# A ninth half tile of transposed keys in the room of the sixth ring slot, and a new pace for the MLP's steps

## The chip, the cores and the metric

One core of one Trainium2 chip. The metric is the device time in microseconds (us). The kernel before takes 1196.23 us (two runs, 1195.41 to 1197.05). Every experiment ran four times beside seven runs of the kernel before on the same chip, whose median was 1195.5 to 1197.2 us in each of the sets. A ratio is the mean time of a kernel's fast runs over that of the kernel before's fast runs of the same rounds, so it is not quite the ratio of the medians that stand beside it; brackets give its 95% interval.

## The reference, cut to what matters

Two layers, and both use the same key and value caches. That is why keys kept on chip from layer 0 save a read in layer 1.

```python
B, Sq, D = 8, 1, 448
Hq, Hkv, Sk, Dh = 16, 8, 4096, 256          # k_cache, v_cache: (8, 8, 4096, 256) bf16
x = A_x
for _ in range(2):
    x = x + attention(layernorm(x), k_cache, v_cache, wq, wo)   # two query heads share a key head
    x = x + block(layernorm(x), w3, w4)   # its input, plus: layernorm, w3, gelu, w4 of it
```

With one position per sequence the shifted mixing in the block contributes nothing, so the kernel needs only w3 and w4. One head's keys are 2 MiB, its values 2 MiB. All heads of both layers would be 512 MiB; this is a problem of reading.

## The kernel before

Keys and values of a (layer, batch, head) come in halves of 1 MiB through a ring of six slots, all issued in one order by SyncE. TensorE transposes keys (a "turn" is four transposes), VectorE and ScalarE copy the result out of PSUM (the memory that TensorE's results land in), TensorE makes the scores and, one head later, the product with the values. A slot is free, and the next read is issued, when TensorE has read the slot.

Eight half tiles of transposed keys (heads 0 to 3) stay on chip from layer 0 to layer 1. Each of the eight periods has a *stretch* of heads with nothing kept, then a *shared group*, in which layer 1 of batch b and layer 0 of batch b+1 alternate over the kept heads:

```python
full = N_KEEP // 2
part = N_KEEP % 2
kept_heads = full + part
A  = lambda b: [(0, b, h) for h in range(kept_heads, HKV)]
Bk = lambda b: [(0, b, h) for h in range(kept_heads)]
C  = lambda b: [(1, b, h) for h in range(kept_heads)]
Dn = lambda b: [(1, b, h) for h in range(kept_heads, HKV)]
first  = [p_ for b in range(1, B) for p_ in A(b)]
second = [p_ for b in range(B - 1) for p_ in Dn(b)]
per = (len(first) + len(second)) / B
# ... each period: per heads of first and second, then C(b)[i], Bk(b + 1)[i] in turn
```

Layer 1 of batch b can't begin before the batch's MLP and its new queries are done (`drain()` finishes them where they are not). That chain, `mix` and then `queries`, is a generator. A `pump()` stands after each turn, each two scores and each product with values, 14 points in a head, and advances it:

```python
def step():
    if jobs:
        n = len(S.ops["pe"])
        # ... next(jobs[0]), or drop the finished job
        return 1.0 if len(S.ops["pe"]) > n else 0.4     # a step with matmuls, or without
    return 1.0

def pump():
    credit["n"] = min(1.0, credit["n"] + credit["rate"]) if jobs else 0.0
    if credit["n"] > 0.0:
        credit["n"] -= step()
# when a batch has finished layer 0:
credit["rate"] = 0.80
jobs.append(mix(b, 1, True))
```

The layernorm is some 26 small VectorE operations in a row, cut by bare `yield`s into steps without matmuls. Each such step before the projection that needs its result lets one pump point of attention pass:

```python
def layernorm(lo, n, twice):
    # ... square, reduce; GpSimd: partition_all_reduce
    yield
    yield
    # ... mean, variance (5 operations)
    yield
    # ... centre; rsqrt: 3 operations, yield, then three Newton steps of 3 operations, each with a yield
# in mix():
    yield from layernorm(lo, n, True)
    scaled(lnT, r_ln, 1, n)
    # ...
    yield
    yield
    for ts in (range(0, 2), range(2, 4), range(4, 7), range(7, 9), range(9, 11), range(11, 14)):
        project(w3_cols, w3_r, C_H, ts, ts[0] >= NF // 2, n)     # TensorE waits for lnT
        # ...
        yield
```

Key copies out of PSUM: turns 1, 3, 5, 7 of a head on ScalarE (`ON_ACT`), the others on VectorE, in the same queue as the layernorm.

Of the kernel before, what the change touches and what calls it, by code (L numbers as in the profile page):

```python
# [18 lines left out]
GELU_K = 0.7978845608028654  # L19
RSQRT_MAGIC = 0x5F3759DF  # L20

N_RING = 6
N_KTR = 4
N_TK = 4
N_KEEP = 8
N_REP = 24
N_MLP = 24
N_PS = 2


# [19 lines left out]
class Sched:  # L50
# [8 lines left out]
    def op(self, eng, fn, reads=(), writes=(), dma=None):  # L59
        o = Op()  # L60
        o.eng, o.fn, o.inc, o.sem, o.amount = eng, fn, False, None, 1
        deps = []
        for r in reads:
            if r.w is not None:
                deps.append((r.w, "raw"))
        for r in writes:
            if r.w is not None:
                deps.append((r.w, "waw"))
            deps += [(t, "war") for t in r.r]
        known = self.known[eng]  # L70
        o.waits = []
        need = {}
        for t, kind in deps:
            if t.key == eng and (eng == "pe" or kind == "war"):
                continue
            if known.get(t.key, -1) >= t.idx:
                continue
            if t.key not in need or need[t.key].idx < t.idx:
                need[t.key] = t
        for t in sorted(need.values(), key=lambda t: -len(t.clock)):  # L80
            if known.get(t.key, -1) >= t.idx:
                continue
            o.waits.append(t)
            t.op.inc = True
            for k, v in t.clock.items():
                if known.get(k, -1) < v:
                    known[k] = v
            known[t.key] = max(known.get(t.key, -1), t.idx)
        if dma is None:
            key, idx = eng, len(self.ops[eng])  # L90
        else:
            key = ("dma", dma)
            idx = self.dsem.setdefault(dma, 0)
            self.dsem[dma] += 1
            o.sem, o.amount, o.inc = dma, 16, True
        o.tok = Tok(key, idx, dict(known), o)
        self.ops[eng].append(o)
        for r in writes:
            r.w, r.r = o.tok, []
        for r in reads:  # L100
            r.r.append(o.tok)
        return o.tok
# [25 lines left out]
def decode_two_layers(nc, A_x, A_k_cache, A_v_cache, A_wq, A_wo, B_w3, B_w4, out):  # L128
# [10 lines left out]
    def sb(name, shape, dt):  # L139
        return nc.alloc_sbuf_tensor(name, shape, dt), Res()  # L140
# [8 lines left out]
    w4, r_w4 = sb("w4_sb", [P, NF, D], bf)  # L149
    ring = [sb(f"ring{i}", [P, HALF, DH], bf) for i in range(N_RING)]  # L150
    ktr = [sb(f"ktr{i}", [P, 4, P], f32) for i in range(N_KTR)]
    keep = [nc.alloc_sbuf_tensor(f"keep{i}", [P, HALF, P], f32) for i in range(N_KEEP)]
    r_keep = [[Res() for _ in range(4)] for _ in range(N_KEEP)]

# [21 lines left out]
    r_o = [Res() for _ in range(B)]  # L176
    pT = [sb(f"pT{i}", [P, NI, 2], bf) for i in range(N_PS)]
    pm = [sb(f"pm{i}", [P, 2], f32) for i in range(N_PS)]
    gm = [sb(f"gm{i}", [P, 2], f32) for i in range(N_PS)]
    nb_ = [sb(f"nb{i}", [P, 2], f32) for i in range(N_PS)]  # L180
    rs = [sb(f"rs{i}", [P, 2], f32) for i in range(N_PS)]
    dn = [sb(f"dn{i}", [P, 2], f32) for i in range(N_PS)]
    rc = [sb(f"rc{i}", [P, 2], f32) for i in range(N_PS)]
# [27 lines left out]
# [5 lines that stand above are left out]
    def kept(h, a):  # L216
        k = 2 * h + a
        return k if k < N_KEEP else None

# [6 lines left out]
    per = (len(first) + len(second)) / B  # L226
# [34 lines left out]
    def load_next():  # L261
        n = state["loaded"]
        if n >= len(chunks):
            return
        state["loaded"] = n + 1
        src, b, h, a = chunks[n]
        t, r = ring[n % N_RING]
        op("sp", lambda e: e.dma_start(
            t[:, :, :], src[b, h].rearrange("(m s) d -> m s d", m=P)[:, a * HALF:(a + 1) * HALF, :]),
           writes=[r], dma=f"ring{n % N_RING}")  # L270

# [3 lines left out]
    def load_rows(t, tf, src, name):  # L275
        parts = []
        w = src.shape[1] // 2
        for kc in range(1, KC):
            parts.append((t[:, kc - 1, :], src[row0(kc):row0(kc + 1), :]))
        for half in range(2):  # L280
            parts.append((tf[64 * half:64 * half + 64, :], src[0:64, w * half:w * half + w]))
        return [op("sp", lambda e, o=o, i=i: e.dma_start(o, i), writes=[Res()], dma=f"{name}{k}")
                for k, (o, i) in enumerate(parts)]

    def reads_of(parts):
        out_ = []
        for t in parts:
            q = Res()
            q.w = t
            out_.append(q)  # L290
        return out_
# [4 lines left out]
    wq_r = reads_of(load_rows(wq, wqf, A_wq, "wq"))  # L296
    for _ in range(2, N_RING):
        load_next()
# [72 lines left out]
    def copies(cols, n):  # L371
        return cols.unsqueeze(1).to_broadcast([cols.shape[0], N_MLP // n, n])

    def room(w, at, n):

        r = N_MLP // n
        return mm[0:w, at:at + r * n].rearrange("p (r n) -> p r n", n=n)
# [49 lines left out]
    def outputs(lo, n, c, ts, first, alone):  # L427

        def f(e):
            w = kr(c)  # L430
            last = None
            for t in ts:
                at = C_Y + c * B + lo
                cols = oT[:, t // 2, t % 2, lo:lo + n]
                last = e.matmul(room(w, at, n) if alone else mm[0:w, at:at + n], wo[:, t, row0(c):row0(c) + w],  # L435
                                copies(cols, n) if alone else cols, start=first and t == ts[0],
                                stop=False, skip_group_check=True)
            return last
        op("pe", f, reads=[r_wo] + [r_o[b] for b in range(lo, lo + n)], writes=[r_mm])
# [58 lines left out]
    credit = {"n": 0.0, "rate": 1.0}  # L498
# [5 lines that stand above are left out]
            try:  # L504
                next(jobs[0])
            except StopIteration:
                jobs.pop(0)
            return 1.0 if len(S.ops["pe"]) > n else 0.4
        return 1.0

    def pump():
        credit["n"] = min(1.0, credit["n"] + credit["rate"]) if jobs else 0.0
        if credit["n"] > 0.0:
            credit["n"] -= step()

    def drain():
# [30 lines left out]
    def attend(g):  # L547
# [5 lines left out]
        def turn(f):  # L553

            a = f // 4
            n = index["k", g, a]
            src, r_src = ring[n % N_RING]
            bank, r_bank = tk[cnt["t"] % N_TK]
# [103 lines left out]
    def pv(g, a):  # L662

        q = g % N_PS
        n = index["v", g, a]
        v, r_v = ring[n % N_RING]

# [14 lines left out]
    def finish(g):  # L682

        layer, b, h = seq[g]
        q = g % N_PS

        def fn(e):
            last = None
            for c in range(2):
                last = e.transpose(pvb[:, DH + c * P:DH + (c + 1) * P], ob[:, c * P:(c + 1) * P], ident4[:, :])  # L690
            return last
        op("pe", fn, reads=[r_ob, r_ident4], writes=[r_pv])
        op("dve", lambda e: e.tensor_reduce(
            os_[:, :].rearrange("p (j c) -> p j c", c=2),
            pvb[:, DH:2 * DH].rearrange("p (c k w) -> p w c k", c=2, k=4)[:, 0:2, :, :],
            axis=AX.X, op=ALU.add), reads=[r_pv], writes=[r_os])
        op("dve", lambda e: e.tensor_tensor(  # L697
            oT[:, 2 * h:2 * h + 2, :, b], os_[:, :].rearrange("p (j c) -> p j c", c=2),
            rc[q][0][:, :].unsqueeze(2).to_broadcast([P, 2, 2]), ALU.mult),
           reads=[r_os, rc[q][1]], writes=[r_o[b]])  # L700
        after(g)
# [5 lines left out]
    def all_but(h):  # L707

        ts = [t for t in range(32) if t // 4 != h]
        for c in (1, 2, 3, 0):  # L710
            for n in range(0, 28, 14):
                outputs(B - 1, 1, c, ts[n:n + 14], c == 1 and n == 0, False)
                yield

    def after(g):

        layer, b, h = seq[g]
        if g == len(seq) - 2:
            jobs.append(all_but(seq[-1][2]))
        if last_of[layer, b] != g:  # L720
            return
        if layer == 0:
            credit["rate"] = 0.80
            jobs.append(mix(b, 1, True))
        elif b == B - 2:
            jobs.append(mix(0, B - 1, False))
        elif b == B - 1:
            for c in range(KC):
                outputs(B - 1, 1, c, range(4 * h, 4 * h + 4), False, False)
            jobs.append(mix(B - 1, 1, False, False))  # L730
# [89 lines left out]
```

## Time and profile before

| | before |
|---|---|
| time, median | 1196.23 us |
| TensorE / VectorE / ScalarE busy | 81% / 41% / 27% |
| ring transfers of 1 MiB | 256 of values, 192 of keys |
| DMA queue 1, share of 16 engines | 97.9% |
| mean granted TensorE clock | 0.925 |

Busy shares are averages over stretches and groups with different limits, so the prediction below reads them by window. Two views follow. The first is the page's row of TensorE's granted clock, in tenths, in 40 slices of 30 us:

```profile
PEclk8879989899999998999989899998999999899886
```

The second is who TensorE waits for inside a layernorm. The columns are microseconds in total, times, and the longest:

```profile
PE ps L598 <- DVE sm L324: 17.6, 20, 1.1
PE mm L405 <- DVE t L364: 13.1, 8, 5.0
...
PE mm L405 <- DVE lnT L364: 9.1, 1, 9.1
```

The reader is to see that each wait is short: 17.6 us over 20 waits, none above 1.1. (The 9.1, and the 5.0 in the row above it, belong to the start and the end of the kernel, where there is no attention to put in between.)

### The profile page before, as it was taken

How to read it: one execution, taken by the hardware profiler on the slowest of the kernel's cores; microseconds unless marked ns; L12 is line 12 of the kernel's file. 1: busy time of each engine (PE TensorE's matmuls, PEld its weight loads, DVE VectorE, ACT ScalarE, POOL GpSimd, SP SyncE). 2: the span in 40 equal slices, each digit the busy share in tenths (PEclk: the TensorE clock that was granted, in tenths of full speed). 3: DMA queues.
4: the chain of work that ended last, by engine and by line, in shares of the span. 5: the costliest groups of instructions: out<-in, count | busy, mean ns of one | idle time of the engine just before them, and what ended most of it. 6: DMA issues, size and time to landing. Idle time of an engine off the chain costs nothing.

```text
span 1196.6 us, 42443 instructions
## 1 busy us (share of the span) xinstructions
PE 963.4 (81%) x19195; PEld 842.2 (70%) x19195; DVE 485.2 (41%) x1707; ACT 320.9 (27%) x907; POOL 104.9 (9%) x281
## 2 busy tenths in 40 slices
PE   2767898788877888788977897788878897789895
PEld 2666787677766777677866886677767786678784
DVE  2323443335433443335433443335433443345253
ACT  1222322232222222232322322222322232223130
POOL 0000001101011001100110001000110011000100
PEclk8879989899999998999989899998999999899886
DMA  9999999999999999999999999999999999999992
GB/s 352 388 412 420 419 416 415 420 419 418 417 421 412 415 403 419 420 419 400 409 420 419 414 401 420 418 421 398 410 420 420 418 407 420 420 419 408 397 393 92
DMA packets 71828, 483.06 MB, mean 404 GB/s; under 512 B 7376, under 2 KB 13408, under 8 KB 13920
## 3 DMA queue, kind: packets, MB, share of 16 engines
q1 hardware_dynamic: 71648, 480.36, 97.9%
q8 instruction: 150, 2.46, 0.8%
q14 instruction: 30, 0.25, 0.0%
HBM read 480.32 MB, written 0.01 MB: 401 GB/s over the span
## 4 chain that ended last, share of the span: by engine, by line
DMA 44%; PE 39%; DVE 10%; issue 5%; POOL 1%; ACT 1%; SPq 0%; POOLq 0%; ACTq 0%
DMA ring<-in_A_k_cache_dram 44%; PE tk L574 21%; PE ps L598 6%; PE pvb L672 4%; PE mm L405 4%; DVE ktr L581 3%; PE mm L485 2%; PE mm L435 1%; PE pvb L690 1%; DVE sm L343 1%; ACT ktr L579 1%; DVE sm L325 1%; POOL gm L648 1%; DVE sm L326 1%; DVE ob L678 1%
## 5 line engine op out<-in xcount | busy, mean ns | idle before, releaser
L574 PE MATMUL tk<-ident,ring 128*128 128x128 f32 x3072 | 458.3, 298 | 121.9 <-DMA ring<-in_A_k_cache_dram 120.4
L574 PEld LDWEIGHTS tk<-ident,ring 128*128 128x128 f32 x3072 | 368.1, 152 | 160.4 <-DMA ring<-in_A_k_cache_dram 147.9
L581 DVE COPY ktr<-tk 128x512 f32<-128x512 f32 x256 | 176.7, 690 | 258.3 <-PE tk L574 257.6
L579 ACT COPY ktr<-tk 128x512 f32<-128x512 f32 x256 | 148.3, 586 | 358.3 <-PE tk L574 358.2
L672 PE MATMUL pvb<-ring,pT 128*2 128x256 bf16 x4096 | 161.7, 279 | 35.9 <-DMA ring<-in_A_v_cache_dram 28.5
L598 PE MATMUL ps<-qT,ktr 128*128 128x48 bf16 x4096 | 145.4, 184 | 22.6 <-DVE sm L324 17.6
L598 PEld LDWEIGHTS ps<-qT,ktr 128*128 128x128 bf16 x4096 | 130.5, 97 | 34.1 <-DVE ktr L581 26.0
L581 DVE COPY keep<-tk 128x512 f32<-128x512 f32 x128 | 88.5, 691 | 155.3 <-PE tk L574 154.7
L654 ACT ACTIVATE pT<-ps,nb 128x32 bf16<-128x32 f32 x256 | 76.4, 298 | 259.3 <-DVE nb L650 212.0
L598 PE MATMUL ps<-qT,keep 128*128 128x48 bf16 x4096 | 139.6, 186 | 5.1 <-issue 4.4
L598 PEld LDWEIGHTS ps<-qT,keep 128*128 128x128 bf16 x4096 | 130.4, 99 | 18.2 <-issue 10.3
L579 ACT COPY keep<-tk 128x512 f32<-128x512 f32 x128 | 75.0, 586 | 232.5 <-PE tk L574 232.5
L672 PEld LDWEIGHTS pvb<-ring,pT 128*2 128x2 bf16 x4096 | 76.0, 82 | 61.0 <-DMA ring<-in_A_v_cache_dram 35.2
L648 POOL PARTITION_ALL_REDUCE gm<-pm x128 | 45.4, 355 | 778.3 <-DVE pm L645 778.3
L678 DVE COPY ob<-pvb 128x256 f32<-128x256 f32 x128 | 53.7, 419 | 46.9 <-PE pvb L672 46.3
L659 POOL PARTITION_ALL_REDUCE dn<-rs x128 | 51.0, 399 | 150.9 <-ACT pT L654 150.9
L645 DVE TENSOR_REDUCE pm<-ps 128x2 f32<-128x64 f32 x128 | 28.6, 224 | 87.8 <-PE ps L598 87.8
L435 PE MATMUL mm<-oT,wo_sb 128*128 128x24 bf16 (+5 forms) x1280 | 60.6, 183 | 1.4 <-DVE oT L697 0.5
L435 PEld LDWEIGHTS mm<-oT,wo_sb 128*128 128x128 bf16 (+1 forms) x1280 | 51.3, 102 | 12.6 <-issue 9.1
L690 PE MATMUL pvb<-ident,ob 128*128 128x128 f32 x256 | 55.8, 302 | 2.8 <-DVE ob L678 1.6
L405 PE MATMUL mm<-lnT,wq_sb 128*128 128x24 bf16 x864 | 48.6, 184 | 10.5 <-DVE lnT L364 9.1
L405 PEld LDWEIGHTS mm<-lnT,wq_sb 128*128 128x128 bf16 x864 | 42.0, 99 | 19.2 <-DVE lnT L364 10.5
(65 smaller groups left out, 474.7 us busy)
## 6 DMA issues: line engine op xcount, KB each, us to landing
ring<-in_A_v_cache_dram SPq DMA_DIRECT2D x256, 1024.0 KB, 12.7
ring<-in_A_k_cache_dram SPq DMA_DIRECT2D x192, 1024.0 KB, 12.4
wo_sb<-in_A_wo_dram SPq DMA_DIRECT2D x1, 3584.0 KB, 26.8
wq_sb<-in_A_wq_dram SPq DMA_DIRECT2D x3, 1024.0 KB, 11.5
w_sb<-in_B_w_dram SPq DMA_DIRECT2D x1, 1568.0 KB, 22.8
w_sb<-in_B_w_dram SPq DMA_DIRECT2D x3, 448.0 KB, 14.3
wqf_sb<-in_A_wq_dram SPq DMA_DIRECT2D x2, 256.0 KB, 15.2
w3f_sb<-in_B_w_dram SPq DMA_DIRECT2D x2, 112.0 KB, 15.3
```

Source lines behind the costliest of these rows:

```text
L405: last = e.matmul(room(P, at + t * B, n), cols(kc, t), copies(rhs, n), start=(kc == 1), stop=(kc == 0), skip_group_check=True)
L435: last = e.matmul(room(w, at, n) if alone else mm[0:w, at:at + n], wo[:, t, row0(c):row0(c) + w], copies(cols, n) if alone else cols, star ...
L574: last = e.transpose(bank[:, j * P:(j + 1) * P], src[:, 4 * (f % 4) + j, :].bitcast(f32), ident4[:, :])
L579: op("act", lambda e: e.copy(flat, bank[:, :]), reads=[r_bank], writes=[r_kt])
L581: op("dve", lambda e: e.tensor_copy(flat, bank[:, :]), reads=[r_bank], writes=[r_kt])
L598: last = e.matmul(pst[:, at:at + 2 * N_REP].rearrange("p (r j) -> p r j", j=2), kt(i, c), repeated(qT[:, b, c, 2 * h:2 * h + 2]), start=(c ...
L648: op("pool", lambda e: e.partition_all_reduce(gm[q][0][:, :], pm[q][0][:, :], P, ReduceOp.max), reads=[pm[q][1]], writes=[gm[q][1]])
L654: return e.activation(pT[q][0][:, :, :].rearrange("p i j -> p j i")[:, j, :], pst[:, C_S:C_S + 2 * NI].rearrange("p (i j) -> p j i", j=2)[ ...
L659: op("pool", lambda e: e.partition_all_reduce(dn[q][0][:, :], rs[q][0][:, :], P, ReduceOp.add), reads=[rs[q][1]], writes=[dn[q][1]])
L672: last = e.matmul(pvb[at:at + 2, 0:DH], pT[q][0][:, a * HALF + i, :], v[:, i, :], start=(a == 0 and i < 4), stop=(a == 1 and i >= HALF - 4 ...
L678: op("dve", lambda e: e.tensor_copy(ob[:, :], pvb[:, 0:DH]), reads=[r_pv], writes=[r_ob])
L690: last = e.transpose(pvb[:, DH + c * P:DH + (c + 1) * P], ob[:, c * P:(c + 1) * P], ident4[:, :])
```

## The change

It gives the room of the sixth slot to a ninth kept half tile, so head 4's first half of keys is read once per batch and not twice. Five heads then take part in the shared groups, so the stretches have 5.25 heads on average in place of 7, and the MLP's steps are paced to fit. With `while`, one pump point runs steps as long as credit is left, so cheap steps (0.4 each) follow one another with no attention between them.

```diff
-N_RING = 6
+N_RING = 5
-N_KEEP = 8
+N_KEEP = 9
+CHAIN = 60
 def pump():
     credit["n"] = min(1.0, credit["n"] + credit["rate"]) if jobs else 0.0
-    if credit["n"] > 0.0:
+    while credit["n"] > 0.0:
         credit["n"] -= step()
-            credit["rate"] = 0.80
+            credit["rate"] = CHAIN / (14 * (per - 1))
```

## The prediction

> **What bounds the kernel now.** I read the page's slices and queues first. One core reads 480 MB; if the DMA engines never rest, nothing else can set the time.
>
> ```profile
> PE   2767898788877888788977897788878897789895
> ...
> DMA  9999999999999999999999999999999999999992
> GB/s 352 388 412 420 419 416 415 420 419 418 417 421 412 415 403 419 420 419 400 409 420 419 414 401 420 418 421 398 410 420 420 418 407 420 420 419 408 397 393 92
> ...
> q1 hardware_dynamic: 71648, 480.36, 97.9%
> ...
> ring<-in_A_v_cache_dram SPq DMA_DIRECT2D x256, 1024.0 KB, 12.7
> ring<-in_A_k_cache_dram SPq DMA_DIRECT2D x192, 1024.0 KB, 12.4
> ```
>
> The reader should see a DMA row of nines and a rate of 415 to 421 GB/s in most slices. 448 transfers of 1 MiB go through the ring. A transfer at 420 GB/s takes 1.0486 MB / 420 = 2.50 us; the landing records in the trace are 2.48 us apart, with a pause of about 1.5 us every 60 us. So 448 x 2.48 = 1111 us, plus 16 to 18 pauses (25), plus 10.4 MB of weights (25), plus start and tail (35 together), is the 1196 us. The landing takes 12.4 us, five transfers' worth: with six slots, a request finds about five ahead of it.
>
> Next, the waits and groups: who waits for whom.
>
> ```profile
> L574 PE MATMUL tk<-ident,ring 128*128 128x128 f32 x3072 | 458.3, 298 | 121.9 <-DMA ring<-in_A_k_cache_dram 120.4
> ...
> L672 PE MATMUL pvb<-ring,pT 128*2 128x256 bf16 x4096 | 161.7, 279 | 35.9 <-DMA ring<-in_A_v_cache_dram 28.5
> ```
>
> TensorE waits 149 us in all for data. But not everywhere. The busy times of windows show two regimes: 12 us of pure attention, 58 us in which a batch's MLP and next queries are mixed in, and the following 70 us, mostly with kept keys.
>
> ```profile
> 378.00:390.00 12.00, 9.18 (x162) 8.31 (x161) 5.40 (x13) 4.08 (x10) 0.88 (x3) 1.00 1.01 423
> 390.00:448.00 58.00, 51.69 (x1068) 44.99 (x1065) 27.12 (x108) 15.97 (x43) 4.56 (x12) 0.97 1.00 408
> 450.00:520.00 70.00, 52.88 (x1061) 45.77 (x1050) 25.04 (x78) 19.27 (x60) 7.53 (x20) 0.93 1.01 419
> ```
>
> The columns are the window, its length, busy us of PE, weight load, VectorE, ScalarE, GpSimd, then clock, DMA share and GB/s. PE is busy 77% of the first, 89% of the second (and stalled on VectorE in part of the rest), 76% of the third. In the middle one PE is slightly slower than the DMA. The DMA rides over it only because five transfers are queued.
>
> The timeline of one layernorm inside that window shows where PE loses time:
>
> ```profile
> 405.16 0.15 DVE L450 TENSOR_TENSOR xx<-mm,xx 128x4 f32<-128x4 f32 x1
> ...
> 405.81 0.40 POOL L339 PARTITION_ALL_REDUCE sm<-sm  x1 [7.01 <-DVE sm L335]
> ...
> 409.64 0.68 DVE L581 COPY ktr<-tk 128x512 f32<-128x512 f32 x1
> ...
> 410.39 0.57 PE L598 MATMUL ps<-qT,ktr 128*128 128x48 bf16 x16 [0.68 <-DVE sm L324]
> ...
> 411.89 0.17 DVE L364 TENSOR_TENSOR lnT<-xc,sm 128x4 bf16<-128x4 f32 x1
> ...
> 412.11 0.25 PE L405 MATMUL mm<-lnT,w_sb 128*128 128x24 bf16 x3 [1.16 <-DVE t L364]
> ```
>
> From the sum into x at 405.16 to the first projection at 412.11 is 7 us. PE stalls only 0.68 + 1.16 = 1.84 us of it, because attention work was placed in between.
>
> **What the Trainium skill says.** "DMA: Bandwidth & Descriptors", section Bandwidth, puts the fabric ceiling at 435 GB/s; the trace's 420 is near it, so fewer bytes is the only way to be quicker. The same page, "Anatomy of one DMA", gives each transfer a fixed cost of about 2 us beside its bytes, mostly the receipt before the semaphore fires (for the GpSimd path). The trace agrees for SyncE's: the first ring transfer, on an empty queue, landed 5.1 us after its issue, 2.5 of it data, so 2.6 fixed. "Perfetto Trace Analysis", section Optimizing Scalar/DVE Operations, gives a VectorE instruction on SBUF about 60 ns fixed cost, and about twice that as profiled latency; here a four-element operation takes 150 to 170 ns and the next starts some 0.19 us after it. So a layernorm is priced by its count of operations.
>
> **The change part by part.**
>
> (1) Ninth kept half tile. The fifth head's first half of keys is read in layer 0 and not again in layer 1: eight transfers less, one per batch. 8 x 2.48 = 19.8 us, with its share of the pauses 20. PE also drops 8 x 16 transposes and VectorE and ScalarE 16 copies each; PE waits for DMA there, so that is worth nothing more. Alone: 1196 - 20 = 1176.
>
> (2) Five slots in place of six. The room is equal (8 KiB a partition each). The rate is not touched while PE waits for data. What shrinks is how far PE may fall behind before the DMA runs dry. In pure attention a key transfer lands 12.8 us after its issue; with five slots that becomes 12.8 - 2.5 = 10.3. The DMA is dry at 5.1 (empty queue); 6.4 us occurs near 1134 and 1155 us with little loss, so I put dry at 5.6. The slack falls from 7.2 to 4.7 us.
>
> (3) The sequence. With five shared heads, the stretch between two shared groups has 5.25 heads on average instead of 7 (counted from the lists: 5,5,6,5,5,6,5,5). The MLP starts after the second head's first turns, so a stretch of five offers 10 + 3 x 14 = 52 pump points, 3.7 heads, where the MLP now takes 172 transposes / 32 = 5.4 heads.
>
> (4) The pump. The rate becomes 60 / (14 x 4.25) = 1.008, capped at 1 credit, and `if` becomes `while`. A step with a matmul costs 1, one without 0.4. There are 46 with (16 + 6 + 8 + 16) and some 23 without. Before, each step without took a point of its own: 46 / 0.8 + 23 = 80 at most, 75 measured (5.4 x 14). Afterwards 46 + 23 x 0.4 = 55 points: it just fits. But the nine empty steps of a layernorm, which were there to put attention between VectorE's chain and the projection, now take about 3 points instead of 9. One point is 7.6 / 14 = 0.54 us of PE work. Some 2 us instead of 5 cover a chain of 7 us, so the stall grows by about 2.7 us, twice per batch, and by about 0.9 at the gelu (one point instead of three): 6.3 us.
>
> **Sum for one stretch.** PE per streamed head without MLP: 9.18 / 12 x 9.92 = 7.6 us (9.92 us is four transfers). Before: 58 us less 1.1 of waiting for DMA is 57, less 5.4 x 7.6 = 41, leaves 16 us for the MLP with its stalls. DMA needed 5.4 x 9.92 = 53.5 us, so PE fell 3.5 us behind, inside the slack of 7.2. After: 3.7 x 7.6 + 16 + 6.3 = 50.4 us against 3.7 x 9.92 = 36.7: 13.7 us behind, against a slack of 4.7. The DMA rests 9 us in each of eight stretches, 72 us. The following shared group can't return this: the DMA already runs at full rate there. If half of the added stall is hidden (work shifts into it, less is queued on VectorE), 6 us a stretch, 47 in all. I take 7 us, 56 in all, a little under the full sum: 1196 - 20 + 56 = 1232; I predict 1230.
>
> **The rivals.** A: bytes alone count, the lag stays under the slack: 1176. For it: DMA at 97.9%, and PE's average load of 81% leaves room over a whole period. Against it: the ring bridges 5 us, a stretch is 50 us long, and the MLP's work is now denser by a third. B: the shorter ring and stretch matter, but the layernorm stalls don't grow: lag 3.7 x 7.6 + 16 - 36.7 = 7.4, dry for 2.7 us a stretch, 22 in all: 1198, no change. For it: VectorE is busy only 47% of the window, so the chain may get through sooner. C: the full sum, 1249. For it: VectorE works in order and has copies between, and PE too is in order, so nothing passes a waiting projection. I believe something between B and C.
>
> **Range and chances.** Low 1192: B with slightly more slack. High 1254: C with a further stall. 2% is 1172 and 1220. Faster needs more than all the bytes saved: 0.03. Within 2% holds A, B and weak forms of C: 0.35. Slower: 0.62.
>
> **What would show it.** Key transfers 184 instead of 192, landing at about 10 us: step 1 and 2. Dips in GB/s once a stretch to 300 to 350, and no dips in the shared groups: the dry DMA. PE's waits for the layernorm (scores after VectorE's sm 17.6 us, projections after t 13.1 us, 31 together) risen to 60 or more: step 4. SyncE's waits for slots still on PE. If GB/s stays at 415 and more throughout and the waits on layernorm don't rise, A is right and I am wrong; if the waits rise and GB/s doesn't fall, I have mis-sized the slack.

## The result, and the profile after

1261.28 us (two runs, 1258.35 and 1264.2), ratio 1.0544 [1.0434, 1.0653]: slower, by 65 us, though it reads 8.4 MB less. From the page of the changed kernel:

```profile
PE   2777887787886887877887888787777887787885
...
PEclk7879888888989989898889888897988988998886
DMA  8999989998999989999999989998999989998982
GB/s 316 378 415 420 374 322 398 420 404 295 384 419 419 371 335 421 419 419 355 358 421 419 378 307 418 421 419 308 399 420 420 401 319 421 420 414 295 362 312 122
...
q1 hardware_dynamic: 70496, 471.97, 93.5%
...
ring<-in_A_v_cache_dram SPq DMA_DIRECT2D x256, 1024.0 KB, 10.1
ring<-in_A_k_cache_dram SPq DMA_DIRECT2D x184, 1024.0 KB, 10.3
```

The reader is to see the row of GB/s: where it had stayed at 397 or more between start and end, it now dips to 295 to 358 about once per period of 140 us, and again near the end (312). The queue's share falls from 97.9% to 93.5%. Key transfers are 184 and take 10.3 us from issue to landing, 2.1 less than before; the ring has one slot (2.48 us) less. The granted clock's row has more eights than before; its mean fell to 0.885.

TensorE's waits for the layernorm, same columns as above:

```profile
PE mm L406 <- DVE lnT L365: 42.9, 10, 11.6
...
PE mm L406 <- DVE t L365: 31.3, 9, 5.0
...
PE mm L486 <- DVE hT L477: 10.1, 10, 1.5
```

Taken away 11.6 us at the start, the first two rows are 62.6 us, twice the 30.7 of before, and single waits are now 3.5 us. One of them, in the timeline (start, length, what, and in brackets the idle time before it and what ended it):

```profile
424.95 0.17 DVE L451 TENSOR_TENSOR xx<-mm,xx 128x4 f32<-128x4 f32 x1 [0.83 <-PE mm L436]
...
426.90 0.68 DVE L582 COPY ktr<-tk 128x512 f32<-128x512 f32 x1
...
430.18 0.18 DVE L365 TENSOR_TENSOR lnT<-xc,sm 128x4 bf16<-128x4 f32 x1
...
430.42 0.25 PE L406 MATMUL mm<-lnT,w_sb 128*128 128x24 bf16 x3 [3.49 <-DVE t L365]
...
430.86 1.11 PE L575 MATMUL tk<-ident,ring 128*128 128x128 f32 x4
```

From the sum into x at 424.95 to the projection at 430.42 is 5.5 us. Some 2 us of attention lie in between, and then TensorE stands for 3.49 us. In the last row four transposes take 1.11 us; at 420.56, before the wait, they took 0.63. The windows around that wait say why (window, length, busy us of PE, weight load, VectorE, ScalarE, GpSimd, then granted clock, DMA share, GB/s):

```profile
413.00:424.00 11.00, 10.84 (x249) 9.71 (x246) 3.90 (x11) 3.20 (x9) 0.75 (x2) 1.00 1.02 412
...
427.00:430.00 3.00, 0.00 (x0) 0.00 (x0) 2.58 (x16) 0.12 (x1) 0.00 (x0) 1.00 1.00 407
430.00:434.50 4.50, 4.08 (x90) 3.70 (x91) 1.54 (x7) 0.58 (x1) 0.35 (x1) 0.62 0.69 246
434.50:438.00 3.50, 2.59 (x45) 2.30 (x42) 2.54 (x9) 1.47 (x6) 0.40 (x1) 1.00 1.01 407
```

TensorE is idle from 427 to 430 while VectorE works; then the granted clock is 0.62 for the next window, and in that same window the DMA falls to 69% and 246 GB/s: by now TensorE is so late in freeing slots that the queue has run empty.

**Where the time went.** I took the landing of each of the 440 ring transfers from the trace and called "lost" what an interval between two landings has above 2.48 us. Before, 63.7 us are lost in all: 32.9 at the start, 29.9 in recurring pauses, 0.9 elsewhere. After, 150.1: 35.4 at the start, 27.9 in pauses, 66.5 in the first seven stretches (with 15 us after each, since landings come after issues), and 20.3 in the last stretch and the end. So the balance is -8 x 2.48 = -19.8 for the bytes, and +86.4 for DMA rest: +66.6, against 65.8 in the two profiled spans (1262.4 and 1196.6). Nearly all of it is lost at transfers that found less than 3.7 us of queued work ahead of them when issued.

### The profile page after: what moved, and what is told of

The parts are those of the page before. It is cut to its first block, busy times and chain, and to the rows that moved or that the text cites. A ratio compares the mean times of both kernels' runs of the same rounds, so it can differ in the third digit from the quotient of the medians.

```text
span 1262.4 us, 42152 instructions
## 1 busy us (share of the span) xinstructions
PE 975.7 (77%) x19067; PEld 857.2 (68%) x19067; DVE 483.6 (38%) x1691; ACT 314.7 (25%) x891; POOL 104.9 (8%) x281
## 3 DMA queue, kind: packets, MB, share of 16 engines
q1 hardware_dynamic: 70496, 471.97, 93.5%
## 4 chain that ended last, share of the span: by engine, by line
PE 44%; DMA 41%; DVE 9%; issue 4%; POOL 1%; SPq 1%; ACT 0%; POOLq 0%; ACTq 0%
DMA ring<-in_A_k_cache_dram 39%; PE tk L575 20%; PE ps L599 9%; PE pvb L673 5%; PE mm L406 4%; PE mm L436 2%; DMA ring<-in_A_v_cache_dram 2%; PE pvb L691 2%; DVE ktr L582 2%; PE mm L486 1%; SPq L269 1%; DVE sm L326 1%; DVE sm L327 1%; DVE sm L344 1%; DVE sm L325 1%
## 5 line engine op out<-in xcount | busy, mean ns | idle before, releaser
L582 DVE COPY ktr<-tk 128x512 f32<-128x512 f32 x224 | 154.6, 690 | 244.8 <-PE tk L575 244.3
L580 ACT COPY ktr<-tk 128x512 f32<-128x512 f32 x224 | 131.2, 586 | 404.4 <-PE tk L575 404.4
L582 DVE COPY keep<-tk 128x512 f32<-128x512 f32 x144 | 99.5, 691 | 170.2 <-PE tk L575 169.6
L599 PE MATMUL ps<-qT,keep 128*128 128x48 bf16 x4608 | 157.0, 187 | 5.6 <-DVE qT L423 3.6
L599 PEld LDWEIGHTS ps<-qT,keep 128*128 128x128 bf16 x4608 | 148.3, 99 | 17.7 <-issue 7.7
L580 ACT COPY keep<-tk 128x512 f32<-128x512 f32 x144 | 84.3, 586 | 266.3 <-PE tk L575 266.3
L599 PE MATMUL ps<-qT,ktr 128*128 128x48 bf16 x3584 | 135.4, 188 | 0.6
L599 PEld LDWEIGHTS ps<-qT,ktr 128*128 128x128 bf16 x3584 | 122.5, 100 | 6.7 <-ACT ktr L580 1.5
L691 PE MATMUL pvb<-ident,ob 128*128 128x128 f32 x256 | 58.4, 314 | 6.1 <-DVE ob L679 6.1
L436 PEld LDWEIGHTS mm<-oT,wo_sb 128*128 128x128 bf16 (+1 forms) x1280 | 52.1, 104 | 13.9 <-issue 10.1
## 6 DMA issues: line engine op xcount, KB each, us to landing
ring<-in_A_v_cache_dram SPq DMA_DIRECT2D x256, 1024.0 KB, 10.1
ring<-in_A_k_cache_dram SPq DMA_DIRECT2D x184, 1024.0 KB, 10.3
```

Of the source, the lines that this page charges most:

```text
L436: last = e.matmul(room(w, at, n) if alone else mm[0:w, at:at + n], wo[:, t, row0(c):row0(c) + w], copies(cols, n) if alone else cols, star ...
L580: op("act", lambda e: e.copy(flat, bank[:, :]), reads=[r_bank], writes=[r_kt])
L582: op("dve", lambda e: e.tensor_copy(flat, bank[:, :]), reads=[r_bank], writes=[r_kt])
L599: last = e.matmul(pst[:, at:at + 2 * N_REP].rearrange("p (r j) -> p r j", j=2), kt(i, c), repeated(qT[:, b, c, 2 * h:2 * h + 2]), start=(c ...
L691: last = e.transpose(pvb[:, DH + c * P:DH + (c + 1) * P], ob[:, c * P:(c + 1) * P], ident4[:, :])
```

## The experiments

For all of them I use two numbers from the traces. The **lag** is the length of the MLP's part of a stretch, less what the DMA needs for the heads transposed in it (9.92 us a head), mean of the first seven stretches: how far TensorE falls behind. **Dry** is the time lost at transfers that found less than 3.7 us of queue ahead. Theory 1 says that dry time comes when the lag exceeds the ring's slack; theory 2, that five outstanding transfers alone slow the DMA; theory 3, that the layernorm waits of the new pump reach the end by themselves.

Lag and dry are of the one profiled execution of each kernel, the medians of all its executions. The pump's rate is 0.80 where the table says so; else it follows the changed kernel's formula, 1.008 with nine tiles and 60/84 = 0.71 with eight (while_r6, r5_while); k9_spread has 1.0.

| kernel | slots | kept | pump | other edit | median us | ratio [95%] | lag | dry |
|---|---|---|---|---|---|---|---|---|
| before | 6 | 8 | if, 0.80 | | 1196 | 1 | 4.5 | 1 |
| r5_only | 5 | 8 | if, 0.80 | | 1203.1 | 1.0055 [1.0029, 1.0080] | 3.9 | 4 |
| while_r6 | 6 | 8 | while | | 1203.8 | 1.0058 [1.0040, 1.0077] | 5.8 | 2 |
| r5_while | 5 | 8 | while | | 1225.3 | 1.0249 [1.0218, 1.0280] | 5.5 | 18 |
| k9_r6_if | 6 | 9* | if | | 1193.9 | 0.9970 [0.9953, 0.9988] | 8.6 | 9 |
| k9_if | 5 | 9 | if | | 1210.4 | 1.0111 [1.0075, 1.0147] | 8.9 | 30 |
| k9_r6 | 6 | 9* | while | | 1236.4 | 1.0354 [1.0311, 1.0397] | 13.9 | 61 |
| k9_r8 | 8 | 9* | while | | 1196.3 | 0.9998 [0.9980, 1.0016] | 13.6 | 15 |
| after | 5 | 9 | while | | 1261.3 | 1.0544 [1.0434, 1.0653] | 14.6 | 87 |
| k9_ln1 | 5 | 9 | while | one Newton step | 1232.3 | 1.0305 [1.0288, 1.0323] | 10.9 | 51 |
| k9_warm | 5 | 9 | while | idle matmuls | 1254.2 | 1.0482 [1.0462, 1.0501] | 13.4 | 69 |
| k9_spread | 5 | 9 | prices turned | | 1216.3 | 1.0169 [1.0142, 1.0195] | 10.1 | 33 |
| k9_nowait | 5 | 9 | while | constant input* | 1257.4 | 1.0518 [1.0493, 1.0544] | 13.6 | 79 |
| k9_nowait2 | 5 | 9 | while | and no lift* | 1224.1 | 1.0240 [1.0217, 1.0263] | 9.9 | 40 |
| k9_nowait3 | 5 | 9 | while | and copies on ScalarE* | 1187.0 | 0.9917 [0.9895, 0.9938] | 5.2 | 10 |
| k9_if_ln1 | 5 | 9 | if | one Newton step | 1188.9 | 0.9927 [0.9911, 0.9944] | 5.7 | 12 |
| k9_if_ln1_act | 5 | 9 | if | and 6 of 8 copies on ScalarE | 1185.3 | 0.9906 [0.9878, 0.9935] | 5.1 | 10 |
| k9_if_ln1_act8 | 5 | 9 | if | and 8 of 8 | 1181.5 | 0.9875 [0.9856, 0.9895] | 4.4 | 5 |
| before_ln1_act | 6 | 8 | if, 0.80 | one Newton step, 6 of 8 | 1194.4 | 0.9987 [0.9971, 1.0004] | 3.3 | 0 |

A star marks a kernel that is wrong on purpose. The comparison with the reference passed all of them, the wrong ones too, so "correct" says little here.

### The parts one by one: r5_only, k9_if, while_r6, k9_r6

**r5_only**, the kernel before with five slots:

```diff
-N_RING = 6
+N_RING = 5
```

> The kernel before with five slots and nothing else changed (eight kept tiles, old pump). Theory 1 (TensorE's lag against the ring's slack): the lag of a stretch stays 4 to 6 us, the slack with five slots is about 4 (10.3 us from issue to landing, dry at about 6.3), so the DMA is dry 0 to 2 us a stretch, some 10 us in all: 1200 to 1210. Theory 2 (five outstanding transfers alone slow the DMA everywhere): most of the 66 us is here, plus the 20 us of bytes not saved: 1260 to 1285. Theory 3 (the layernorm stalls of the while pump are the cause): 1196, nothing.

Measured 1203.1 us. Its row of GB/s, to be held against that of the changed kernel:

```profile
GB/s 356 390 415 420 419 400 419 420 419 396 403 420 420 410 399 391 420 419 406 406 419 420 416 413 420 417 416 397 418 419 420 398 403 420 420 419 394 394 405 104
```

There are shallow dips (391 to 406) and none at 300. Five slots alone cost 7 us, in the range of theory 1, where theory 2 asked for 64 or more. Theory 2 falls.

**k9_if**, the changed kernel with the old conditional:

```diff
-    while credit["n"] > 0.0:
+    if credit["n"] > 0.0:
```

> The changed kernel with if in place of while in the pump: one empty step per point again, what is left over is drained. Theory 1: the added stall of some 4 us a stretch goes, over eight stretches and the tail about 30 us: 1225 to 1240. Theory 2: no change, 1260. Theory 3: the whole loss goes and the bytes show: 1176 to 1190.

Measured 1210.4: 51 us of the 65 are gone, more than theory 1 had expected (the lag fell by 5.7 us, not by the 4 of the waits alone), but the bytes still don't show. Theory 3 in its pure form is wrong too. The trace also shows what `if` does to a chain that no longer fits its stretch: in five of the first seven stretches the last 120 matmuls of the queries (15 of 16 steps) run in one block of 3.4 to 3.9 us at the end, left over for `drain()`, where the changed kernel has 24 in such a block. So this kernel keeps the layernorms spread and not the matmuls.

**while_r6**, the new pump with six slots and eight tiles:

```diff
-N_RING = 5
-N_KEEP = 9
+N_RING = 6
+N_KEEP = 8
```

> Six slots, eight kept tiles, only the new pump (while, rate 60/84 = 0.71). Theory 1: the lag of a stretch grows from about 4 to about 8 us against a slack of 6.5: dry 1 to 2 us a stretch, 1200 to 1210. Theory 2: 1196. Theory 3: 4 us of stall in each of eight stretches reach the end: 1225 to 1235.

Measured 1203.8: the same `while` that costs 51 us above costs 7 here, where the stretch is longer, the ring has a slot more and the rate is 0.71 in place of 1.008; this pair doesn't separate the three.

**k9_r6**, a sixth slot for the changed kernel. It doesn't fit in SBUF, so the ninth tile uses the first one's room:

```diff
-N_RING = 5
+N_RING = 6
-keep = [... for i in range(N_KEEP)]
+keep = [... for i in range(N_KEEP - 1)]
+keep.append(keep[0])          # and the same for r_keep
```

> The changed kernel with a sixth slot, which fits only because the ninth kept tile shares the room of the first (the result is wrong on purpose; times, transfers and instructions are those of the change). Theory 1: 2.5 us more slack in each of eight stretches and the tail, 20 to 25 us back: 1235 to 1242. Theory 2: all comes back, 1176 to 1182. Theory 3: nothing comes back, 1261.

Measured 1236.4: 25 us back for 2.5 us of slack in eight stretches. Theory 1's number.

### Threshold and dose: k9_r8, r5_while, k9_ln1, k9_spread

**k9_r8** has eight slots, with three shared tiles:

```diff
-N_RING = 5
+N_RING = 8
+keep += keep[:3]              # of six tiles; r_keep likewise
```

> The changed kernel with eight slots (three of the nine kept tiles share room with the first three; wrong result on purpose). Theory 1, lag against slack: the slack rises from about 4 to 11.5 us against a lag of about 14, so 2 to 3 us a stretch stay dry: 20 to 25 us over the floor of 1176, so 1192 to 1205. If instead the stalls themselves lengthened the whole and not by way of the ring, it would stay near the 1236 of six slots.

Measured 1196.3. The lag is still 13.6 us and TensorE's waits for the layernorm still stand (the three rows of the result differ by 2 us at most), but the DMA hardly feels them until the last slices:

```profile
GB/s 348 406 395 420 419 396 412 419 419 416 385 420 420 419 402 421 419 419 419 378 419 419 419 377 409 420 419 407 408 419 420 419 398 416 420 419 412 353 334 75
```

So a wait of TensorE costs nothing by itself; only what exceeds the ring's slack costs.

**r5_while** asks whether costs add or a threshold lies between:

```diff
-N_KEEP = 9
+N_KEEP = 8
```

> Five slots and the new pump, but eight kept tiles (the long stretch). Five slots alone cost 7 us and the pump alone 7. If the costs only add: 1210. Theory 1 has a threshold in it: six slots had some slack left that each change used up, so together they cost more than the sum: lag 7 us against a slack of 4, 3 us in each of eight stretches: 1218 to 1228.

Measured 1225.3. Five slots (7 us) and the pump (7 us) together cost 29, twice their sum. The pump costs 7, 29 - 7 = 22, 42 (1236.4 - 1193.9) and 51 us as slack and stretch shrink: a threshold. (The first two are at the rate of 0.71, against 0.80 with `if`.)

**k9_ln1** shortens the chain on VectorE by six operations a layernorm and keeps the pump's steps:

```diff
 for i in range(3):
+    if i > 0:
+        yield
+        continue
```

> The changed kernel with one Newton step in place of three in each inverse square root (six VectorE operations of some 0.19 us fewer in each layernorm; the steps of the pump are the same, the result slightly less exact). If the chain on VectorE behind the first projection is what TensorE waits for, each of two layernorms a batch is 1.1 us shorter, and in eight dry stretches and the tail all of it reaches the end: 15 to 25 us less, 1237 to 1246. If the loss of the while pump is in the bunching of its matmuls and not in the chain, nothing: 1258 to 1264.

Measured 1232.3, 29 us less, beyond the expected 15 to 25. The summed waits for VectorE of a stretch fell from 7.8 to 5.4 us as reckoned (12 x 0.19), the lag by 3.7. The rest goes with the clock: integrating 1 minus the granted clock over a stretch gives 6.6 us in the changed kernel and 3.9 here, part of it lying in the waits themselves.

**k9_spread** turns the prices of steps round:

```diff
-    return 1.0 if len(S.ops["pe"]) > n else 0.4
+    return 0.5 if len(S.ops["pe"]) > n else 1.0
-credit["rate"] = CHAIN / (14 * (per - 1))
+credit["rate"] = 1.0
```

> The changed kernel with the pump's prices turned round: two steps with matmuls at one point (0.5 each), one step without at each point (1.0), 46 points in all, so that the chain fits in a stretch of 52 points with the layernorms still spread. Theory 1: the added stall goes and nothing is left to drain; the lag falls to about 7 to 8 us against a slack of 4: 1200 to 1212, near or below the if variant's 1210. If matmuls bunched in pairs hurt, above 1215.

Measured 1216.3, a miss: the waits for VectorE fell to 4.5 us a stretch, but the chain was through after 3.1 heads, not the 3.6 of the changed kernel. The same MLP beside less streaming is a larger lag, some 1.2 us by an estimate (half a head, 9.92 us of DMA less the prediction's 7.6 of TensorE, for each head), of a lag of 10.1. The other reading, that matmuls in pairs hurt, is not excluded by this run alone; k9_nowait3 below speaks against it.

### The clock, the last corner and two attempts at a better kernel

**k9_warm** puts 96 matmuls of 24 columns ahead of a projection that waits:

```diff
+def warm(k):
+    # k times: matmul(mm[:, 440:464], ident, ident[:, 0:24])
 # in mix, and in queries for one batch, ahead of the projections:
+    warm(96)
```

> The changed kernel with 96 idle matmuls (24 columns, into unused columns) put ahead of each batch's first projection after a layernorm, where TensorE only waits for VectorE. They take about 2.7 us of a wait of 3.5. If the lower granted clock after each long stall (0.55 to 0.62 for some 4.5 us in the trace) is a part of the cost of its own, it goes: about 2 us at each of 16 stalls, 25 to 35 us less, 1226 to 1237. If the stall itself is the whole cost, nothing changes: 1258 to 1266.

Measured 1254.2: 7 us, where 25 to 35 were expected if the clock mattered and none if not. The timeline shows two stalls of one stretch:

```profile
421.14 2.55 PE L405 MATMUL mm<-ident 128*128 128x24 bf16 x96
...
424.42 0.65 PE L589 MATMUL tk<-ident,ring 128*128 128x128 f32 x4
...
438.66 2.55 PE L405 MATMUL mm<-ident 128*128 128x24 bf16 x96
442.30 0.25 PE L417 MATMUL mm<-lnT,wq_sb 128*128 128x24 bf16 x3 [1.08 <-DVE lnT L365]
...
442.75 1.11 PE L589 MATMUL tk<-ident,ring 128*128 128x128 f32 x4
```

After the first filler the transposes run at 0.65 us a turn; after the second, with an idle 1.08 us behind it, they are slow again, 1.11. In all, transposes of more than 400 ns within the first seven stretches are 145 of 804 in the changed kernel, 85 of 804 here and 20 of 848 in k9_if (counted beside the MLP). So the filler mended about half of what the new pump added to the slow clock. Whether the slow clock has a cost of its own stays open: the ratio here, 1.0482, lies inside the interval of the changed kernel's two runs (1.0434 to 1.0653), so the 7 us are not clear of the noise. If they are real, 7 us for 60 of 145 would make some 17 us for all, an estimate.

**k9_r6_if**: k9_r6 with `if` in the pump.

> Nine kept tiles (the ninth sharing room with the first, wrong on purpose), six slots, if in the pump: the last corner of the three parts. Lag about 8 us against a slack of 6.5: 1 to 2 us a stretch dry, over the floor of 1176: 1185 to 1195. If the costs of the parts only added (while 51, the sixth slot 25 against the change's 1261), 1185; if the short stretch by itself costs what 1210 minus 1176 shows whatever the ring, 1210.

Measured 1193.9, in the range, and the first with nine tiles that is clearly below the kernel before. Its profiled span (1188.8 us) shows 76.2 us lost in all, 12.5 more than before, of which 9 are dry queue; so of the 20 us of bytes some 7 arrive there.

**k9_if_ln1**: two edits on the changed kernel.

```diff
-    while credit["n"] > 0.0:
+    if credit["n"] > 0.0:
-    for i in range(3):          # Newton steps of the inverse square root
+    for i in range(1):
```

> The changed kernel with if in the pump and one Newton step (with its empty pump steps gone too, so less is left to drain). Attempt at a kernel that beats both. The lag of the if variant (7 to 8 us) falls by about 2 to 3: 3 to 4 us, at the slack of 4; what remains is the start and the last stretch: 1188 to 1198.

Measured 1188.9. **k9_if_ln1_act** adds `ON_ACT = (1, 2, 3, 5, 6, 7)`:

> The same, with six of the eight key copies of a head on ScalarE in place of four, so that fewer copies queue on VectorE behind and between a layernorm's operations. If what is left of the stall comes from that queue: 1182 to 1192. If ScalarE's copies of 0.59 us, three in four turns, now make TensorE wait for a bank, 1195 or more.

Measured 1185.3. Both are below the kernel before, as expected.

### Is the wait all of the pump's cost? k9_nowait, k9_nowait2, k9_nowait3

**k9_nowait** lets the projections of a single batch, and the lift of 64 rows behind the first one, read a constant tile that nothing writes, in place of `lnT`:

```diff
-    rhs = lnT[:, ...]
+    rhs = (fix if n == 1 else lnT)[:, ...]      # the same in lift(); reads r_fix in place of r_ln
```

> The changed kernel whose projections of a single batch read a constant tile in place of the layernorm's result (wrong on purpose; all VectorE work and all matmuls stay), so TensorE no longer waits for the layernorms. If waits for the layernorm, with the slow clock after them, are what the while pump costs, the lag falls from 14.6 to 4 or 5 us, near the slack: 1183 to 1197. If the denser matmuls of the new pump cost by themselves, 1210 (the if variant) or more.

Measured 1257.4: nothing, and taken at its word that would have refuted the waits. But the waits had not gone:

```profile
PE mm L408 <- DVE lnT L398: 59.4, 17, 4.7
```

The second projection now waited 3.6 us for VectorE's copy of the lifted rows. That copy reads the same PSUM bank, and it stands in VectorE's queue behind the whole layernorm. An in-order queue carries a wait to everything behind it.

**k9_nowait2** drops the lift and its copy for a single batch (`if n == 1: return`).

> As k9_nowait, which did not take the wait away: TensorE then waited 3.6 us for VectorE's copy of the lifted rows, which reads the same PSUM bank and stands behind the whole layernorm in VectorE's order. Here the lift and its copy go too for a single batch (wrong on purpose). If waits for the layernorm, with the slow clock after them, are what the while pump costs: lag 14.6 to 5 or 6 us, 1183 to 1200. If the denser matmuls of the new pump cost by themselves: 1210 or more.

Measured 1224.1, in the range of the second cause (1210 or more): by its number the density would be guilty. But the projection's wait is gone and a third way opened: the attention's own scores wait for key copies that stand behind the layernorm,

```profile
PE ps L604 <- DVE ktr L587: 32.0, 16, 2.8
```

which is some 4 us a stretch. **k9_nowait3** puts all eight key copies on ScalarE:

> As k9_nowait2, with all eight key copies of a head on ScalarE. In k9_nowait2 TensorE no longer waited for the projection's data but 4.2 us a stretch for key copies that stand behind the layernorm on VectorE. With both ways closed: if those waits are the rest of the while pump's cost, the lag falls from 9.9 to 5 or 6 us, 1190 to 1202. If ScalarE, now with all copies, holds TensorE back (0.59 us a copy against 0.68 us a turn), or the matmuls' density costs by itself: 1210 or more.

Measured 1187.0, a little below the expected range, with the `while` pump untouched; the remaining wait for copies is

```profile
PE ps L604 <- ACT ktr L585: 2.7, 7, 0.4
```

So the density of the matmuls costs nothing that shows. What the new pump cost was TensorE standing behind bunched VectorE work, by three ways, with the slower clock after it. One thing is missing: the same edits with the `if` pump were not run. They took away 74 us, more than the pump's 51, so they also mended waits that k9_if has, and a few us of density could hide behind that.

### The best version and its control

**k9_if_ln1_act8** is k9_if_ln1 with `ON_ACT = (0, 1, 2, 3, 4, 5, 6, 7)`.

> The best variant so far (if, one Newton step, six of eight copies on ScalarE, 1185) with all eight copies on ScalarE. If what is left (lag 5.1 us) still comes from copies behind the layernorm: 1180 to 1185. If ScalarE becomes the engine that TensorE waits for: 1188 or more.

Measured 1181.5, 1.2% below the kernel before, which is clear of the noise, and some 5.5 us above the floor of 1176 that the prediction had for the bytes alone. Its page:

```profile
PEclk8879998899899998999899998999889999999896
DMA  9999999999999999999999999999999999999992
GB/s 357 385 414 420 419 389 420 419 420 418 379 419 420 419 419 408 419 420 410 378 419 419 412 393 422 419 420 417 416 411 419 414 404 417 419 420 417 367 398 106
```

The DMA row is nines again; single slices at 367 to 393 remain. TensorE's waits for the layernorm are down to one each:

```profile
PE mm L406 <- DVE lnT L365: 7.3, 1, 7.3
...
PE mm L406 <- DVE t L365: 3.9, 1, 3.9
```

**before_ln1_act** is the control: the two edits of k9_if_ln1_act (except the pump, which is the old one there anyway) on the kernel before.

> The kernel before (six slots, eight kept tiles, old pump) with one Newton step and six of eight copies on ScalarE: the control for the 1185 us of the nine-tile kernel with the same two edits. If the ninth tile earns the gain there, this stays at the DMA's bound, 1192 to 1197. If the shorter layernorm and the copies earn it, 1184 to 1189.

Measured 1194.4, against 1185.3 with nine tiles and the same edits. The gain is the ninth tile's; the edits only let it through. (No control was run for the copies 8 of 8.) The control is bound by the DMA already, so shorter waits have little to give. One Newton step is a loss of accuracy, from rounding level to about 0.2% in the inverse square root by the formula, which whoever takes this version must accept; no run here tried two steps.

## Why the prediction was right or wrong

The direction and the mechanism were right, the time was outside the range: 1261, predicted 1230, range 1192 to 1254. By its own steps:

1. **The bytes** (-20 us). Right: 184 key transfers, and the rest of the balance closes with -19.8.
2. **The slack** (7.2 us to 4.7). Nearly right. Landing took 10.3 us as stated. Dry began a little earlier than 5.6 us from issue to landing: transfers that found less than about 3.7 us ahead of them, so about 6.2, already came late (in the changed kernel those that found 3.0 to 3.5 landed 3.1 us after the one before in the median, in place of 2.48). That makes the slack 4.1.
3. **The shorter stretch.** Right: 3.6 heads measured beside the MLP, 3.7 predicted. (That the chain "just fits" was not: by the prediction's own count it needs 55 points, and a stretch of five heads has 52. In those stretches the last 24 query matmuls run in a row at the end, in 0.8 us.)
4. **The pump.** The size was right, its terms were not, and that is luck. Added wait predicted 6.3 us a stretch; measured 7.8 in place of 3.9, so 3.9. Against k9_if, which has the same stretch and ring, the lag rose by 5.7: the waits for VectorE by 2.9 (4.9 to 7.8), the clock lost over a stretch by 3.9 (2.6 to 6.6), partly within the same waits. The clock was left out of the sum; that it fills the gap is read from the traces, and k9_warm didn't settle it. The Trainium skill, "TensorE: Matmul & The Clock Gate", in Part 1 on the HAM clock gate, says that the clock halves after an idle window of about 3.4 us and that the same time of activity brings it back. The trace agrees at this stall: 3.49 us idle, then 0.62 granted, turns of 1.11 us in place of 0.63. It also shows slow turns after shorter waits (last section). I had read the clock's row and not priced it.
5. **The lag** (13.7 us). Measured 14.6.
6. **From the lag to the time.** Here the prediction failed. Its full sum, rival C, had 9 us a stretch; I took 7, "if half of the added stall is hidden (work shifts into it, less is queued on VectorE)", a discount that no view of the profile supported. The first seven stretches lost 66.5 / 7 = 9.5 us each, where the measured lag less the measured slack is 14.6 - 4.1 = 10.5: hardly anything was hidden. And I priced the last stretch as one of eight equal ones; it and the end, with the MLP of the last batch and then that of the other seven batches together, where the shared group has values only, lost 20.3 us. Seven stretches at 9.5 for 7 are 17.5 us more, 20.3 for 7 in the last is 13, the start 2.5: 33 us on the sum of 1232, less 3 in the pauses and elsewhere, where the profiled run took 1262.

Of the rivals, A (bytes alone) is what k9_if_ln1_act8 nearly reaches, and B (waits that don't grow, 1198) is nearest to k9_if, with waits of 4.9 us a stretch: 1210. (Two small slips in the sums change nothing: the full sum C is 1176 + 72 = 1248, not 1249, and the weights are 10.6 MB, not 10.4.)

## What to carry to other kernels

In a kernel that the DMA bounds, a buffer slot is worth nothing until the consumer's longest lag needs it, and then each microsecond of missing slack is paid in every period: compare the lag of the worst stretch with the slack before trading a slot for bytes, and treat the end of the program as a stretch of its own. Where an in-order engine waits behind a chain of small operations, spread other work between, shorten the chain, or take unrelated work out of the queue behind it; and when an experiment that removes a wait changes nothing, look whether the wait is still there by another way. Don't discount a sum without a view that shows where the discount comes from.

## What the Trainium skill lacked or had wrong

- "TensorE: Matmul & The Clock Gate", Part 1, tells what brings the clock back, and that frequent short idles can make it swing, but not how thin activity may be. In k9_warm, 96 matmuls of 24 columns over 2.55 us, then 1.08 us idle, were followed by slow turns (1.11 us) at one stall, while the same filler, with 0.30 us idle after it, was followed by fast ones (0.65 us) at the other. And the kernel before has 97 of 1217 slow transposes beside the MLP in its first seven stretches, with no wait for VectorE above 1.2 us there (for data up to 1.9). The page has no measure by which to foresee these; whether its remark in Part 4, that transposes don't count as busy in the same way, bears on them, no run here tests.
- "DMA: Bandwidth & Descriptors" gives the fixed cost of a transfer, but not how much must be queued to keep the engines from resting. Here, on SyncE's queue with 1 MiB transfers, it was about 3.7 us of queued work (some one and a half transfers of 2.48 us); a transfer issued on an empty queue landed 5.0 us later.
- No page has the recurring pause in an otherwise full stream: mostly 1.1 to 1.7 us more than usual between two landings, about every 60 us, some 30 us of the 1196 in all.
